# A last scan behind the products with its gates, and a load behind a score: one reordering in an mLSTM and mixture-of-experts kernel

## The chip, the cores and the metric

The kernel runs on one core of one Trainium2 chip. The metric is device time in microseconds (us) of one execution. TensorE (PE) does the matrix products, VectorE (DVE), ScalarE (ACT) and GpSimd (POOL) the elementwise work, and SyncE (SP) issues the transfers between device memory and the core.

## The reference

The inputs are those of an mLSTM layer (2 batches, 8 heads, 768 steps, head size 40) and of a mixture of 4 experts that runs on its output (1536 tokens of 320 values, hidden size 1024).

```python
for t in range(S):
    m_new = np.maximum(f_gate[:, :, t] + m, i_gate[:, :, t])
    f_stab = np.exp(f_gate[:, :, t] + m - m_new)
    i_stab = np.exp(i_gate[:, :, t] - m_new)
    C = f_stab * C + i_stab * outer(v[t], k[t])
    n = f_stab * n + i_stab * k[t]
    y[t] = sigmoid(o_gate[t]) * (C @ q[t]) / np.maximum(np.abs(n @ q[t]), 1.0)
x = y as (tokens, heads * head size)
p = domain_probs / domain_probs.sum(-1)
for e in range(4):
    out += p[:, e] * (np.maximum(x @ w1[e], 0) @ w2[e])
```

## The kernel before, in words

The recurrence is worked in chunks of 128 steps. A chunk of one batch has a number n (n = 0 and 1 are the two batches' first chunk, 2 and 3 their second, and so on), and the chunks 2j and 2j+1 are pair j; there are six pairs. Inside a chunk the work is split into two halves of 64 steps. For pair j the steps are, by the names in the code:

- `load_f` brings the forget factors of a pair from device memory into the tile `fb`, four transfers a pair; `decay(n)` is a scan of VectorE that makes of `fb` the running products `dd` of chunk n. The scan reads `fb` and a constant, `id8`, both in SBUF.
- `values(n)` and `keys(n)` are GpSimd products of the loaded tile `vk` (scaled values `vp`, scaled keys `kp`); `keys(n)` needs the scan of chunk n.
- `scores` are products on TensorE; `weigh(j)` multiplies them on VectorE by `dd` into `pm`, in two halves.
- `carry`, `state` and `keep` pass the state `cs` on: GpSimd, TensorE and VectorE in turn.
- `inter(j)` forms on TensorE the part of the output that comes from the state (`y1`, line 556) and scales it by the decay into `yb`. For j = 1 alone the scaling is split: one VectorE instruction (line 562) for half 0, and eight ScalarE instructions (line 571) for half 1. `intra(j)` forms the part inside the chunk (`y0`, line 596).
- `norms(j)` adds `yb` to `y0` (line 603), makes the denominator (line 604), multiplies by the output gates in `acc` (line 607, tile `xm`), and its second part, `norm(...)`, divides (lines 611 to 654) into `xr`. `gate_o(j)` is the sigmoid on ScalarE that makes those gates, line 390.
- `turn(j)` transposes `xr` on TensorE (tile `px`, line 662) and stores it as `xst`, the input of the experts (ScalarE lines 665 and 666, VectorE lines 669 and 670).

`steps(n)` puts n steps of the first expert between these: a hidden block (TensorE line 157, ScalarE line 166, VectorE line 170) or an output block (TensorE line 204). From about 100 us on only the experts are left.

Nothing reorders this: each engine runs its instructions in the order in which the code emits them, and waits, in order, for what they need. SyncE too issues its transfers in the order of the code. `behind(ap)` is a tiny transfer (line 710, to `mark`) that reads `ap`; SyncE waits until `ap` is written, and so all later transfers stand behind it.

The change touches `inter` and the first round, j = 1, of the loop over pairs. In it `decay(b + 2)` is the scan of chunk 5 (that of chunk 4 stands ahead of the loop), `keys(b + 2)` the keys of chunk 5, and `load_f(3)` the factors of chunks 6 and 7, whose scans run in the round after.

Of the kernel before, what the change touches and what calls it, by code (L numbers as in the profile page):

```python
# [15 lines left out]
B, H, S, D = 2, 8, 768, 40  # L16
NE, DM, FF = 4, 320, 1024
NT = B * S
L = 128
# [4 lines left out]
NP = H // 2  # L24
# [20 lines left out]
def tile_mlstm_moe(ctx, tc, g0, g1, qk, vk, ot, dp, w1, w2, out):  # L45
    ctx.enter_context(tc.manual_schedule())
    nc = tc.nc
# [175 lines left out]
    with ExitStack() as actx:  # L223
# [50 lines left out]
        bT = const.tile([L, 2, NC, B * NP], F32, name="bT")  # L274
# [119 lines left out]
        fbs, dds, vvs, pms, ss, sts = {}, {}, {}, {}, {}, {}  # L394
# [26 lines left out]
        def load_f(j):  # L421
            for n in (2 * j, 2 * j + 1):
                b, c = n % B, n // B
                fbs[n] = fb = a0.tile([L, H, C], F32, tag="fb", name="fb")
                for u in range(2):
                    nc.sync.dma_start(
                        fb[hs[u]].rearrange("p h t -> p (h t)"),
                        f_d[2 * c - 4 + u:2 * c - 3 + u, b * H * C:(b + 1) * H * C].to_broadcast(
                            [C, H * C]
                        ),  # L430
                    )
# [7 lines left out]
        def decay(n):  # L439
            b, c = n % B, n // B  # L440
            if c:
                if not b:
                    d = a1.tile([L, B, H, C], F32, tag=f"dd{c % 2}", name="dd")
                    dds[n], dds[n + 1] = d[:, 0], d[:, 1]
                    dds[c, "pair"] = d
                scan(dds[n], fbs.pop(n), id8)
                return
            dds[n] = a1.tile([L, H, L], F32, tag=f"dd{n}", name="dd")
            for i, f in enumerate(fbs.pop(n)):
                scan(dds[n][:, 4 * i:4 * i + 4], f, id4)  # L450
# [8 lines left out]
        def keys(n):  # L459
            nc.gpsimd.tensor_mul(  # L460
                kp[n % 2][:, :, 0:D], vks[n // 2][:, n % 2, 1],
                dds[n][:, :, (C if n // B else L) - 1:].to_broadcast([L, H, D]),
            )
# [49 lines left out]
        def cst(j, u):  # L513
            return cs[(2 * j + u) % 3]
# [32 lines left out]
        def inter(j, eng=nc.scalar):  # L547

            y1 = ps_a.tile([L, 2, B, NP, C], F32, tag="a", name="y1")
            for n in (2 * j, 2 * j + 1):  # L550
                b = n % B
                for p in range(NP):
                    for r in range(2):
                        q = slice(64 * r, 64 + D * r)
                        for u in (r, 1 - r):
                            nc.tensor.matmul(  # L556
                                y1[hs[u ^ r], r, b, p, 0:D + 1], qT(n)[q, p, hs[u]],
                                cst(j, u)[q, b * NP + p], start=True, stop=True,
                            )
            yb = ybs[j] = a1.tile([L, 2, B, NP, D + 1], F32, tag="yb", name="yb")  # L560
            if eng is nc.vector:
                eng.tensor_mul(  # L562
                    yb[:, 0].rearrange("t b p d -> t (b p) d"),
                    y1[:, 0].rearrange("t b p d -> t (b p) d")[..., 0:D + 1],
                    bT[:, 0, j].unsqueeze(2).to_broadcast([L, B * NP, D + 1]),
                )
            for b in range(B):
                for p in range(NP):
                    for r in range(eng is nc.vector, 2):
                        i = b * NP + p  # L570
                        nc.scalar.activation(  # L571
                            yb[:, r, b, p], y1[:, r, b, p, 0:D + 1], AF.Copy,
                            scale=bT[:, r, j, i:i + 1],
                        )

        def intra0(b):
            pool, tag = (ps_a, "a") if b else (ps_h, "ph")
# [36 lines left out]
        xms, nqs = {}, {}  # L614
# [87 lines left out]
        def steps(n):  # L702
            for _ in range(n):
                if not work[0].step():
                    work.pop(0)

        def behind(ap):

            i = next(marks)
            nc.sync.dma_start(mark[i:i + 1, 0:ap.shape[-1]], ap)  # L710
# [34 lines left out]
        for r in range(2):  # L745
            for u in range(2):
                t = tri[hs[u], r, hs[u ^ r]]
# [113 lines left out]
        for j in range(1, NG):  # L861
            a, b = 2 * j, 2 * j + 1
            nxt, far = j + 1 < NG, j + 2 < NG
            k = SLOTS[j - 1]
            if j == NG - 2:
                raw1 = raws.tile([L, 3, FF], F32, tag="raw", name="raw1")

            def load(i, ap):
                if far or j == NG - 2:
                    behind(ap)  # L870
                if far:
                    (load_vk, None, lambda j: (load_qk(j), load_o(j)))[i](j + 2)
                elif j == NG - 2:
                    nc.sync.dma_start(raw1[:, i], w1[1, :, i])

            if nxt:
                values(a + 2)
                values(b + 2)
                if j > 1:
                    decays(j + 1)  # L880
                else:
                    decay(b + 2)
                keys(a + 2)
                keys(b + 2)
                steps(1)
            if j == 2:
                gate_o(2)
            norm = norms(j)
            if j == 1:
                behind(xms.pop(j)[0:1, 1, 0, 0:32])  # L890
                load_f(3)
            else:
                load(0, xms.pop(j)[0:1, 1, 0, 0:32])
                steps(1)
            norm(nc.vector if j == 1 else nc.gpsimd)
            if j == 1:
                steps(1)
            if nxt:
                carry(j + 1, 0)
            if j == 1:  # L900
                scores(a + 2)
                scores(b + 2)
                weigh(j + 1)
            steps(k[0] - 1 - nxt)
            if j > 1:
                turn(j)()
            if nxt:
                if j > 1:
                    gate_o(j + 1)
                if j > 1:  # L910
                    scores(a + 2)
                    scores(b + 2)
                hidden = work[0].todo[0][0] == work[0].hidden
                state(j + 1, *((ps_o, "po") if hidden else (ps_h, "ph")))
                if j == 1:
                    low = turn(j)
                keep(j + 1, 0)
                if j == 1:
                    load(0, cst(j + 1, 1)[0:1, 0, 0:32])
                    load_o(2)  # L920
                if not far:
                    load(1, cst(j + 1, 1)[0:1, 0, 0:32])
                low() if j == 1 else weigh(j + 1)
                if far:
                    carry(j + 1, 1)
                    keep(j + 1, 1)
                steps(k[1])
                inter(j + 1)
                load(2, ybs[j + 1][0:1, 0, 0, 0, 0:32])
                intra(j + 1)  # L930
# [113 lines left out]
```

## Time and profile before

| What | Value |
|---|---|
| median of 3 runs | 393.89 us (393.89 to 394.18) |
| the profiled execution | 393.9 us, its span 392.2 us |
| TensorE busy | 385.0 us, 98% of the span |
| VectorE, ScalarE, GpSimd busy | 158.8, 123.7, 94.0 us |
| granted TensorE clock, mean | 0.998 |

The span runs from the first to the last instruction of the profiled execution. Its own time is 1.7 us more. The profile has a timeline of each engine (start, duration, operation and, in brackets, the idle time ahead of it and what ended it), the windows (busy time and transfer rate of a stretch) and a view of one line's instructions. A timeline row that merges several instructions gives their number as x8.

### The profile page before, as it was taken

How to read it: one execution, taken by the hardware profiler on the slowest of the kernel's cores; microseconds unless marked ns; L12 is line 12 of the kernel's file. 1: busy time of each engine (PE TensorE's matmuls, PEld its weight loads, DVE VectorE, ACT ScalarE, POOL GpSimd, SP SyncE). 2: the span in 40 equal slices, each digit the busy share in tenths (PEclk: the TensorE clock that was granted, in tenths of full speed). 3: DMA queues.
4: the chain of work that ended last, by engine and by line, in shares of the span. 5: the costliest groups of instructions: out<-in, count | busy, mean ns of one | idle time of the engine just before them, and what ended most of it. 6: DMA issues, size and time to landing. Idle time of an engine off the chain costs nothing.

```text
span 392.2 us, 8247 instructions
## 1 busy us (share of the span) xinstructions
PE 385.0 (98%) x3584; PEld 350.5 (89%) x3584; DVE 158.8 (41%) x270; ACT 123.7 (32%) x296; POOL 94.0 (24%) x114
## 2 busy tenths in 40 slices
PE   9999899999999999999999999999999999999996
PEld 6899799999989989989889889889889899899896
DVE  7788976665433132142141351241231431321421
ACT  3784644446263231061130240160220420310310
POOL 8988344370463100044100010071000100000000
PEclk9999999999999999999999999999999999999999
DMA  7894574353003220003000040003000001001001
GB/s 224 287 289 163 191 228 160 106 198 104 9 1 134 73 89 2 0 2 134 0 2 0 2 160 2 1 0 135 0 2 0 2 8 43 17 17 52 0 18 50
DMA packets 8717, 28.46 MB, mean 73 GB/s; under 512 B 1354, under 2 KB 2906, under 8 KB 7530
## 3 DMA queue, kind: packets, MB, share of 16 engines
q1 hardware_dynamic: 8682, 27.95, 21.2%
q8 instruction: 28, 0.46, 0.5%
q14 instruction: 7, 0.06, 0.0%
HBM read 25.94 MB, written 2.00 MB: 71 GB/s over the span
## 4 chain that ended last, share of the span: by engine, by line
PE 89%; DVE 5%; POOL 3%; issue 2%; ACT 0%; POOLq 0%; DVEq 0%
PE po L204 41%; PE ph L157 38%; PE ph L187 3%; PE pwm L71 1%; PE y L596 1%; PE s L481 1%; POOL w2s L92 1%; PE px L662 1%; PE y L556 1%; PE fb L416 1%; DVE dd L434 1%; DVE xm L607 1%; POOL vp L456 0%; PE st L529 0%; POOL xr L650 0%
## 5 line engine op out<-in xcount | busy, mean ns | idle before, releaser
L204 PE MATMUL po<-w2s,h 128*128 128x320 f32 x1152 | 172.4, 309 | 0.0
L204 PEld LDWEIGHTS po<-w2s,h 128*128 128x128 f32 x1152 | 169.8, 188 | 1.0
L157 PE MATMUL ph<-xst,w1s 128*128 128x512 f32 (+1 forms) x816 | 163.1, 358 | 0.0
L157 PEld LDWEIGHTS ph<-xst,w1s 128*128 128x128 f32 x816 | 135.8, 189 | 24.3 <-issue 2.4
L166 ACT ACTIVATE h<-ph 128x512 fp32r<-128x512 f32 x96 | 57.4, 598 | 191.0 <-PE ph L157 187.5
L170 DVE SCALAR_TENSOR_TENSOR h<-ph,h 128x512 fp32r<-128x512 f32 x96 | 66.3, 691 | 105.8 <-ACT h L166 105.3
L215 DVE SCALAR_TENSOR_TENSOR acc<-po,pw,acc 128x320 f32<-128x320 f32 x36 | 19.8, 550 | 99.9 <-PE po L204 99.9
L92 POOL TENSOR_TENSOR w1s<-raw,w1s 128x512 fp32r<-128x512 f32 (+1 forms) x24 | 23.5, 1029 | 76.1 <-ACT w1s L89 70.9
L92 POOL TENSOR_TENSOR w2s<-raw,w2s 128x640 fp32r<-128x640 f32 x6 | 9.5, 1576 | 96.2 <-ACT w2s L89 96.2
L434 DVE TENSOR_TENSOR_SCAN dd<-fb,id 128x512 f32<-128x512 f32 x14 | 18.9, 1378 | 1.3 <-POOL kp L460 1.0
L571 ACT ACTIVATE yb<-y,bT 128x41 f32<-128x41 f32 x72 | 14.0, 340 | 4.9 <-DVE yb L562 2.6
L89 ACT ACTIVATE w2s<-raw 128x640 fp32r<-128x640 f32 x12 | 8.8, 733 | 19.3 <-DMA raw<-in_w 19.3
L213 ACT ACTIVATE acc<-po,pw 128x320 f32<-128x320 f32 x12 | 6.3, 527 | 22.2 <-PE po L204 22.2
L456 POOL TENSOR_TENSOR vp<-vk,iT 128x320 f32<-128x320 f32 x12 | 11.1, 944 | 8.8 <-PE y L596 4.2
L650 POOL TENSOR_TENSOR xr<-xm,ni 64x320 f32<-64x320 f32 x9 | 7.6, 848 | 21.5 <-DVE ni L612 21.2
L187 PE MATMUL ph<-xd,w1s 64*128 64x512 f32 x40 | 12.0, 419 | 0.0
L187 PE MATMUL ph<-xst,w1s 64*128 64x512 f32 x40 | 12.0, 418 | 0.0
L89 ACT ACTIVATE w1s<-raw 128x512 fp32r<-128x512 f32 (+1 forms) x24 | 11.2, 517 | 0.0
L460 POOL TENSOR_TENSOR kp<-vk,dd 128x320 f32<-128x320 f32 x12 | 9.8, 827 | 1.3 <-DVE dd L434 1.2
L545 DVE TENSOR_TENSOR cs<-cd,st 40x328 f32<-40x328 f32 x18 | 8.9, 492 | 1.1 <-POOL cd L536 0.7
L187 PEld LDWEIGHTS ph<-xst,w1s 64*128 64x128 f32 x40 | 6.6, 185 | 2.9 <-issue 1.9
L92 DVE TENSOR_TENSOR w2s<-raw,w2s 128x640 fp32r<-128x640 f32 x6 | 5.3, 889 | 9.2 <-ACT w2s L89 9.2
(105 smaller groups left out, 200.7 us busy)
## 6 DMA issues: line engine op xcount, KB each, us to landing
qk<-in_qk SPq DMA_DIRECT2D x4, 1024.0 KB, 4.8
raw<-in_w SPq DMA_DIRECT2D x3, 1280.0 KB, 5.4
vk<-in_vk SPq DMA_DIRECT2D x5, 640.0 KB
raw<-in_w SPq DMA_DIRECT2D x2, 1536.0 KB
qk<-in_qk SPq DMA_DIRECT2D x4, 512.0 KB
fb<-f_d SPq DMA_DIRECT2D x16, 128.0 KB, 6.5
acc<-in_ot SPq DMA_DIRECT2D x6, 320.0 KB, 6.8
out<-acc SPq DMA_DIRECT2D x12, 160.0 KB, 1.8
```

Of the source, the lines that this page charges most:

```text
L89: nc.scalar.activation(hi, raw, AF.Copy)
L92: eng.tensor_sub(lo, raw, hi.bitcast(F32))
L157: nc.tensor.matmul(ph[:, i, :], self.w1s[:, wi, f * L:(f + 1) * L], xst[:, xi, self.t0:self.t0 + n], start=(k == 0 and not self.wide), sto ...
L166: nc.scalar.activation(hh, ph, AF.Relu)
L170: nc.vector.scalar_tensor_tensor(out=hl, in0=ph, scalar=0.0, in1=hh.bitcast(F32), op0=ALU.max, op1=ALU.subtract)
L187: nc.tensor.matmul(self.banks[f][:, 0, :], self.w1s[r, 5, f * L:(f + 1) * L], x, start=True, stop=False,)
L204: nc.tensor.matmul(po, self.hs[f][a][:, sl], ws[:, b, f, :], start=(first and i == 0), stop=(last and i == len(ks) - 1),)
L215: nc.vector.scalar_tensor_tensor(out=acc[:, i, :], in0=po, scalar=pw[:, i, e:e + 1], in1=acc[:, i, :], op0=ALU.mult, op1=ALU.add,)
L434: nc.vector.tensor_tensor_scan(out=out.rearrange("p h t -> p (h t)"), data0=f.rearrange("p h t -> p (h t)"), data1=i.rearrange("p h t -> p ...
L456: nc.gpsimd.tensor_mul(vv[:, :, 0:D], vks[n // 2][:, n % 2, 0], iec.to_broadcast([L, H, D]))
L460: nc.gpsimd.tensor_mul(kp[n % 2][:, :, 0:D], vks[n // 2][:, n % 2, 1], dds[n][:, :, (C if n // B else L) - 1:].to_broadcast([L, H, D]),)
L571: nc.scalar.activation(yb[:, r, b, p], y1[:, r, b, p, 0:D + 1], AF.Copy, scale=bT[:, r, j, i:i + 1],)
```

## The change

It does three things. In `inter`, where the scaling is split, the eight ScalarE instructions are emitted ahead of the VectorE instruction. In round j = 1, `decay(5)` and `keys(5)` move from ahead of `norms(1)` to behind its first part. And `load_f(3)` moves from behind `xm` of pair 1 to behind `pm` of pair 2.

```diff
@@ inter(j, eng)
             yb = ybs[j] = a1.tile([L, 2, B, NP, D + 1], F32, tag="yb", name="yb")
-            if eng is nc.vector:
-                eng.tensor_mul(yb[:, 0] ..., y1[:, 0] ..., bT[:, 0, j] ...)
             for b in range(B):
...
                             yb[:, r, b, p], y1[:, r, b, p, 0:D + 1], AF.Copy,
                             scale=bT[:, r, j, i:i + 1],
                         )
+            if eng is nc.vector:
+                eng.tensor_mul(yb[:, 0] ..., y1[:, 0] ..., bT[:, 0, j] ...)
@@ loop over pairs
                 if j > 1:
                     decays(j + 1)
-                else:
-                    decay(b + 2)
                 keys(a + 2)
-                keys(b + 2)
+                if j > 1:
+                    keys(b + 2)
                 steps(1)
...
             norm = norms(j)
             if j == 1:
-                behind(xms.pop(j)[0:1, 1, 0, 0:32])
-                load_f(3)
+                decay(5)
+                keys(5)
             else:
...
             if j == 1:
                 scores(a + 2)
                 scores(b + 2)
                 weigh(j + 1)
+                behind(pms[a + 2][0:1, 0, 0:32])
+                load_f(3)
```

On VectorE, from the scan of chunk 4 to the division of pair 1, the rows stand as follows before and after. The scan is named SCALAR_TENSOR_TENSOR on line 434 here and TENSOR_TENSOR_SCAN in the trace; `y_633` is `y1`, `y_676` is `y0`.

```order
 L434 SCALAR_TENSOR_TENSOR dd<-fb,id_120 128x512 [waits DMAHW4_49,DMAHW3_49]
-L562 TENSOR_TENSOR yb<-y_633,bT 128x328 [waits PE_49]
-L434 SCALAR_TENSOR_TENSOR dd<-fb,id_120 128x512 [waits DMAHW6_49,DMAHW5_49]
-L603 TENSOR_TENSOR y_676<-y_676,yb 128x16x41 [waits DVE_49,PE_49,Activation_49]
+L570 TENSOR_TENSOR yb<-y_633,bT 128x328 [waits PE_49,Activation_49]
+L603 TENSOR_TENSOR y_676<-y_676,yb 128x16x41 [waits DVE_49,PE_49]
 L604 TENSOR_SCALAR nq<-y_676 128x16 [waits DVE_49]
 L607 TENSOR_TENSOR xm<-y_676,acc 128x640
+L434 SCALAR_TENSOR_TENSOR dd<-fb,id_120 128x512 [waits DMAHW6_49,DMAHW5_49]
 L611 TENSOR_TENSOR y_676<-y_676,nq 128x16 [waits DVE_49]
 L612 RECIPROCAL ni<-y_676 128x16 [waits DVE_49]
```

The second scan moved down past three rows, and the scaling on VectorE now waits for ScalarE's eight, where those waited for it before.

On SyncE, at the end of round j = 1's first half, this is the difference; the four `fb` transfers are those of `load_f(3)`.

```order
 L710 DMA mark<-h 1x32
 L377 DMA qk_132<-in_qk 128x2048
-L710 DMA mark<-xm 1x32
+L710 DMA mark<-pm 1x32
 L426 DMA fb<-f_d 64x512 x4
 L710 DMA mark<-cs_131 1x32
```

The order of SyncE's transfers is the same; what the four loads, and all behind them, wait for has moved from `xm` to the first half of `pm`. The orders of TensorE, ScalarE and GpSimd don't move; on ScalarE the first of the eight waits for TensorE instead of VectorE.

## Rows read from the trace of the kernel before

**Rows 1.** Timeline of TensorE: start, duration, operation, idle time ahead.

```profile
32.45 1.14 PE L556 MATMUL y<-cs,qk 64*64 64x41 f32 x64
...
40.66 0.36 PE L529 MATMUL st<-vp,kp 64*40 64x41 f32 x16 [0.43 <-issue]
41.92 0.85 PE L662 MATMUL px<-ident,xr 128*128 128x128 f32 x6 [0.90 <-DVE xr L650]
...
45.65 1.14 PE L596 MATMUL y<-vp,pm 64*64 64x41 f32 x64 [0.35 <-DVE xst L670]
46.73 8.06 PE L157 MATMUL ph<-xst,w1s 128*128 128x256 f32 x64
54.87 0.87 PE L662 MATMUL px<-ident,xr 128*128 128x128 f32 x6
```

**Rows 2.** Timeline of VectorE, the pair's products and the next pair's xm.

```profile
33.65 1.52 DVE L434 TENSOR_TENSOR_SCAN dd<-fb,id 128x512 f32<-128x512 f32 x1
35.21 0.50 DVE L562 TENSOR_TENSOR yb<-y,bT 128x328 f32<-128x328 f32 x1
35.63 2.75 DVE L434 TENSOR_TENSOR_SCAN dd<-fb,id 128x512 f32<-128x512 f32 x1
38.30 0.82 DVE L603 TENSOR_TENSOR y<-y,yb 128x656 f32<-128x656 f32 x1
...
39.25 0.81 DVE L607 TENSOR_TENSOR xm<-y,acc 128x640 f32<-128x640 f32 x1
...
40.60 0.49 DVE L647 TENSOR_TENSOR xr<-xm,ni 128x320 f32<-128x320 f32 x1
41.10 0.67 DVE L650 TENSOR_TENSOR xr<-xm,ni 64x80 f32<-64x80 f32 x1
41.80 0.69 DVE L499 TENSOR_TENSOR pm<-s,dd 128x512 f32<-128x512 f32 x1
...
51.14 0.81 DVE L607 TENSOR_TENSOR xm<-y,acc 128x640 f32<-128x640 f32 x1
```

**Rows 3.** Timeline of GpSimd beside it.

```profile
35.20 1.40 POOL L456 TENSOR_TENSOR vp<-vk,iT 128x320 f32<-128x320 f32 x2
36.57 0.74 POOL L460 TENSOR_TENSOR kp<-vk,dd 128x320 f32<-128x320 f32 x1
38.52 0.74 POOL L460 TENSOR_TENSOR kp<-vk,dd 128x320 f32<-128x320 f32 x1 [1.22 <-DVE dd L434]
40.71 0.96 POOL L650 TENSOR_TENSOR xr<-xm,ni 64x320 f32<-64x320 f32 x1 [1.45 <-DVE ni L612]
...
48.34 1.09 POOL L456 TENSOR_TENSOR vp<-vk,iT 128x320 f32<-128x320 f32 x1 [3.50 <-DMA vk<-in_vk]
```

**Rows 4.** Source view of line 434: duration in ns, least, median and most.

```profile
L434 DVE TENSOR_TENSOR_SCAN dd<-fb,id x14: 1198/1224/2753, 6.1 to 81.0; 128x512 f32<-128x512 f32 x14
```

**Rows 5.** Timeline of ScalarE: the split scaling, a hidden block, pair 2's sigmoid.

```profile
35.80 1.60 ACT L571 ACTIVATE yb<-y,bT 128x41 f32<-128x41 f32 x8 [2.60 <-DVE yb L562]
...
48.94 0.60 ACT L166 ACTIVATE h<-ph 128x512 fp32r<-128x512 f32 x1 [0.22 <-PE ph L157]
49.44 0.73 ACT L390 ACTIVATE acc<-acc 128x640 f32<-128x640 f32 x1
```

**Rows 6.** Timeline of SyncE's queue: when each transfer was issued.

```profile
40.09 0.24 SPq L710 DMA_DIRECT2D mark<-xm  x1
40.38 2.37 SPq L426 DMA_DIRECT2D fb<-f_d  x4
...
43.86 0.36 SPq L383 DMA_DIRECT2D vk<-in_vk  x1
44.27 0.85 SPq L386 DMA_DIRECT2D acc<-in_ot  x1
```

**Rows 7.** Windows: length; PE, PEld, DVE, ACT, POOL; clock, DMA share, GB/s.

```profile
41.00:48.00 7.00, 5.75 (x157) 5.44 (x155) 6.78 (x14) 5.59 (x26) 2.15 (x3) 1.00 0.69 215
46.00:56.00 10.00, 9.92 (x145) 9.40 (x141) 7.84 (x14) 5.96 (x22) 5.56 (x7) 1.00 0.99 319
```

More of the change, by code (lines that the diff above doesn't have):

```diff
@@ L560, in inter @@
             yb = ybs[j] = a1.tile([L, 2, B, NP, D + 1], F32, tag="yb", name="yb")
-            if eng is nc.vector:
[L562 to L566, printed above, removed]
             for b in range(B):
@@ L574, in inter @@
                         )
+            if eng is nc.vector:
+                eng.tensor_mul(
+                    yb[:, 0].rearrange("t b p d -> t (b p) d"),
+                    y1[:, 0].rearrange("t b p d -> t (b p) d")[..., 0:D + 1],
+                    bT[:, 0, j].unsqueeze(2).to_broadcast([L, B * NP, D + 1]),
+                )
         def intra0(b):
```

## The prediction

> **What bounds the kernel now.** I read the page first: TensorE is busy for 98% of the span, so an edit pays only where TensorE stands idle. Then its timeline around the edit [rows 1]. It waits 0.43 us inside the state products (put down to issue, not to another engine), 0.90 us ahead of the transposes of pair 1 at 41.92 (for VectorE's line 650), and 0.35 us ahead of the next `y0` at 45.65 (VectorE's line 670). From there it is all but full: 9.92 of 10 us in the window from 46 to 56 [rows 7]. So what matters is when VectorE gets through its products between 35 and 45 us, and whether TensorE can then use the time.
>
> VectorE's timeline [rows 2] shows the cause: the scan of chunk 5 takes 2.75 us, from 35.63 to 38.38, where the median of 14 scans is 1.22 us [rows 4]. Beside it GpSimd runs three products without a gap, from 35.20 to 37.31 [rows 3], and the scan ends 1.07 us behind the last of them. So the scan hardly ran until GpSimd stopped; 1.5 us of it is waiting, and the addition of line 603, queued behind it, starts only at 38.30. The Trainium skill states this as a rule ("SBUF — State Buffer", section "Who interferes with whom"): a VectorE instruction with two SBUF inputs and a GpSimd instruction that reads SBUF share an interface, and the later one blocks for the whole of the other. By it the scan would end near 37.31 + 1.22 = 38.53; the trace has 38.38 and agrees.
>
> **The change part by part.** No operation is added or removed; three move.
>
> The eight ScalarE instructions first. Before, ScalarE stood idle for 2.60 us until VectorE's half was written, and began 0.09 us behind its end (35.71 to 35.80) [rows 2, 5]. Now it needs only `y1`, whose products end at 32.45 + 1.14 = 33.59 [rows 1]; with the same 0.09 it begins at 33.68 and ends 1.60 us later, at 35.28. VectorE's half, in turn, now waits for all eight: 35.28 + 0.09 = 35.37, against 35.21 before. This costs 0.16 us on VectorE, with nothing to hide it, since the scan of chunk 4 ends at 35.17. Behind the waiting instruction stands all of VectorE's chain.
>
> The scan behind the products. The half scaling takes 0.50 us, to 35.87. The addition follows at about 35.90 instead of 38.30, and from its start to the end of `xm` it is 40.06 - 38.30 = 1.76 us [rows 2]: 37.66. This stretch overlaps GpSimd's three products, and I cost that at nothing: VectorE's half scaling, which like these instructions takes one operand from PSUM, kept to 0.50 us right beside GpSimd. The upper bound is 1.5 us, what the scan lost. Then the scan, at 37.66, when GpSimd is through at 37.31 and waits for this very scan: 1.22 us, to 38.88. The division's line 647 came 40.60 - 40.06 = 0.54 us behind `xm`; now it is ready 0.54 us behind the scan, at 39.42, 1.18 us earlier.
>
> A part of this goes back at once. The keys of chunk 5 start 0.14 us behind the scan (38.38 to 38.52) and take 0.74 [rows 3]: 39.02 to 39.76, later than before by 0.50. Line 647 reads two SBUF tiles as the scan does, so it may wait for them, till about 39.65 (the scan, too, went on a little ahead of GpSimd's recorded end). From line 647's start to line 650's end it was 1.17 us: 40.82 instead of 41.77. If line 647 isn't held, it is 40.59. I take 40.82, the value by the scan's row: **0.95 us** earlier. The rule of the skill named above speaks against the change here: by it the keys, which start first, hold line 647 to their end; without it the gain would be 1.18 us. GpSimd's part of the division (0.96 us from 39.85) ends by 40.82 as well. The state products, which need these keys, end at 41.02 as before [rows 1]; the transposes can start then, 0.90 us earlier, and the rest of VectorE's row follows without a gap, so the `y0` products come at about 44.7 instead of 45.65.
>
> The load. SyncE's mark waited for `xm`, and issued at 40.09 [rows 6]. Now it waits for the first half of `pm`, which starts with the chain at 41.80 - 0.95 = 40.85 and takes 0.69: 41.54. The mark and four loads then need 42.75 - 40.09 = 2.66 us: to 44.23 instead of 42.75. Behind them in SyncE's queue stand the mark on `cs`, `vk` of pair 3 and the gates `acc` of pair 2. They waited for `cs` until 43.5; now they wait for the loads. With 0.24 us for a mark and some gaps, `vk` is issued near 44.6 instead of 43.86 and `acc` near 45.0 instead of 44.27: **0.75 us** later each. The transfers are themselves short of room: their share is 0.99 from 46 to 56 us, after 0.69 from 41 to 48 [rows 7], so what starts later lands later. I take 0.75 us for the landings; the bounds are 0.3 (what straggles now may then run freely) and 1.45 (the loads' own shift).
>
> Who waits for that? The sigmoid of pair 2, ahead of `xm` at 51.14. `vk` had landed by 48.34, where it ended GpSimd's wait [rows 3]. `acc`, 128 x 640 values of 4 bytes or 328 KB, issued right behind it, needs 1.03 us at the 319 GB/s of the window; from about 48.2 this gives 49.2, between 48.3 and the sigmoid's start at 49.44 [rows 5, 7]. Later by 0.75 this is 49.95; the sigmoid, 0.09 behind it and 0.73 long, ends at 50.77. Without the loads `xm` of pair 2 would start at 51.14 - 0.95 = 50.19. So it starts near 50.80, and the gain there is 0.34 us. The transposes of pair 2 at 54.87 follow from it, TensorE's 8.06 us of hidden blocks having ended earlier: more than half of what TensorE saved it then waits there. GpSimd's four products with `vk` (about 2.9 us from 49.0 on) end at 52.0, just ahead of the division, and cost nothing; without that cover they would cost what they overrun. The factors themselves land by 47.7 now, since their scan of chunk 7 ran at 47.7 without a wait; 1.45 later the scan still ends near 49, when the first hidden block's VectorE part is ready.
>
> **Sum.** 0.95 us less at `y0` of pair 2, 0.6 given back at `xm` of pair 2, 0.35 left. Behind 55 us TensorE is full, so what is left stays to the end: 393.9 - 0.35 = 393.55 for the profiled execution, whose 393.9 is also the median. Something over 0.2% of this, 0.8 us, is about what a measurement can tell from no change; this is less.
>
> **Rivals.** (a) All of it is kept: `acc` lands by 50.19 - 0.73 - 0.09 = 49.37, less than 0.2 us later than now. For it speaks that its landing is read here from bounds a whole us apart; against it, the full transfer engines and the later issue. 393.9 - 0.95 = 392.95. (b) The scan is slow by itself or for another neighbour, such as ScalarE's eight, and takes its 2.75 us wherever it stands: then it ends at 40.41, the keys at 41.29, line 650 at 42.4, 0.6 later than before, and with the loads behind it (`acc` 2.3 later, 51.4, sigmoid to 52.2) `xm` of pair 2 comes 1.1 us late: 395.0. The 13 other scans, of which the median is 1.22, speak against it. (c) Slower by the same block in the next pair: if the factors of chunk 7 land behind `vk` of pair 3, GpSimd's first three products (2.1 us) run ahead of that scan and hold it to 51.2, end 52.4 instead of 48.9; the hidden block's VectorE part and `xm` wait behind it, some 2.8 us: 396.7. It decides when the factors land later than about 49.0; they are issued ahead of `vk`, which speaks against it. (d) The change doesn't do what it says, and the addition still comes late, because ScalarE's eight begin late: 393.9.
>
> **How the numbers follow.** Forecast, with the larger part given back: 0.59, and 393.1 to 394.3 as its own range (landings 0.3 to 1.45 later give a gain of 0.8 to a loss of 0.35, with a little more for the products that TensorE reads next, whose transfer stands in the same queue). (a) 0.23, faster by over 0.2%. (b) 0.07 and (c) 0.06, slower. (d) 0.05, the same. So faster 0.23, same 0.64, slower 0.13. The range takes in (a), the forecast's own range and a little of what lies between it and (b): 392.8 to 394.6.
>
> **What would show it.** Right: the scan of chunk 5 at about 1.2 us, starting near 37.7; the addition near 35.9; ScalarE's eight from 33.7; transposes of pair 1 near 41.0; `fb` loads from 41.8; TensorE idle for some 0.6 us ahead of the transposes of pair 2, put down to the division there, and ScalarE's sigmoid waiting for `acc`. Wrong: a scan over 2 us, line 647 late by a whole chain of GpSimd's, no wait at the sigmoid (then a), or scan 7 stretched beside GpSimd (then c).

## The result, and the profile after

The changed kernel takes 396.85 us, the median of 6 runs (395.35 to 397.44); the kernel before, beside it, 394.16 (6 runs, 393.89 to 394.78). The ratio is 1.0062, with a 95% interval of 1.0043 to 1.0081: slower by 0.6%, where 393.55 was forecast and 394.6 was the upper end of the range. A ratio is estimated over all executions but those more than 1.5% above the fastest of the same kernel (four of twelve in one kernel, with everything early), so it need not be the quotient of the two medians. The profiled execution took 396.73 us, 2.8 more than that of before.

The first half of the forecast came about nearly to the hundredth. VectorE's timeline of the changed kernel (start, duration, operation, idle time ahead and its releaser), which answers to [rows 2]:

```profile
35.33 0.50 DVE L570 TENSOR_TENSOR yb<-y,bT 128x328 f32<-128x328 f32 x1 [0.16 <-ACT yb L565]
35.93 0.85 DVE L603 TENSOR_TENSOR y<-y,yb 128x656 f32<-128x656 f32 x1
...
37.64 1.21 DVE L434 TENSOR_TENSOR_SCAN dd<-fb,id 128x512 f32<-128x512 f32 x1
...
39.26 0.82 DVE L647 TENSOR_TENSOR xr<-xm,ni 128x320 f32<-128x320 f32 x1
40.09 0.67 DVE L650 TENSOR_TENSOR xr<-xm,ni 64x80 f32<-64x80 f32 x1
...
52.73 0.82 DVE L607 TENSOR_TENSOR xm<-y,acc 128x640 f32<-128x640 f32 x1 [2.53 <-ACT acc L390]
53.47 0.68 DVE L170 SCALAR_TENSOR_TENSOR h<-ph,h 128x512 fp32r<-128x512 f32 x1
```

The scan takes 1.21 us instead of 2.75, and line 650 ends at 40.76 (forecast 40.82). The last two rows are the trouble: `xm` of pair 2 comes at 52.73 instead of 51.14 [rows 2], behind an idle stretch of 2.53 us. TensorE's timeline of the same kernel, against [rows 1]:

```profile
40.90 0.85 PE L662 MATMUL px<-ident,xr 128*128 128x128 f32 x6 [0.54 <-DVE xr L650]
...
44.63 1.14 PE L596 MATMUL y<-vp,pm 64*64 64x41 f32 x64 [0.35 <-DVE xst L670]
45.70 6.01 PE L157 MATMUL ph<-xst,w1s 128*128 128x256 f32 x48
54.21 3.11 PE L157 MATMUL ph<-xst,w1s 128*128 128x256 f32 x16 [2.49 <-DVE h L170]
57.12 1.48 PE L662 MATMUL px<-ident,xr 128*128 128x128 f32 x6
```

At the `y0` products TensorE is 1.02 us ahead of before (44.63 against 45.65). Then the 64 products of the four hidden blocks, which ran as one row of 8.06 us, break after the third block for 2.49 us, and what follows is slow: 3.11 us for the fourth block, 1.48 for transposes that took 0.87. These start 2.25 us later than before (57.12 against 54.87) and last 0.61 longer, together 2.86 us: all of the loss. What the break waits for is told by the chain of waits (start, length, what) in that stretch:

```profile
45.19 6.75 DMA acc<-in_ot
...
51.96 0.74 ACT acc L390
...
52.73 0.82 DVE xm L607
53.55 0.61 DVE h L170
...
54.21 3.11 PE ph L157 x16
```

The gates of pair 2 are issued at 45.19 and land 6.75 us later. ScalarE's sigmoid waits for them, VectorE's `xm` for the sigmoid, the second hidden block's VectorE part stands behind `xm` in VectorE's row, and TensorE's fourth block needs that. ScalarE's timeline shows the same, against [rows 5]:

```profile
33.70 1.60 ACT L565 ACTIVATE yb<-y,bT 128x41 f32<-128x41 f32 x8 [0.52 <-PE y L556]
...
47.92 0.60 ACT L166 ACTIVATE h<-ph 128x512 fp32r<-128x512 f32 x1 [0.22 <-PE ph L157]
51.96 0.74 ACT L390 ACTIVATE acc<-acc 128x640 f32<-128x640 f32 x1 [3.45 <-DMA acc<-in_ot]
52.60 1.07 ACT L166 ACTIVATE h<-ph 128x512 fp32r<-128x512 f32 x2
```

And SyncE's queue, against [rows 6], shows the gates issued 0.92 us later (45.19 against 44.27):

```profile
41.51 0.24 SPq L710 DMA_DIRECT2D mark<-pm  x1
41.80 2.38 SPq L426 DMA_DIRECT2D fb<-f_d  x4
44.28 0.40 SPq L710 DMA_DIRECT2D mark<-cs  x1
44.77 0.36 SPq L383 DMA_DIRECT2D vk<-in_vk  x1
45.19 0.42 SPq L386 DMA_DIRECT2D acc<-in_ot  x1
```

The slow products are told by the windows (length; PE, PEld, DVE, ACT, POOL busy; granted clock, DMA share, GB/s):

```profile
51.70:54.20 2.50, 0.02 (x1) 0.00 (x0) 1.47 (x3) 1.71 (x3) 2.39 (x4) 1.00 0.99 333
54.00:55.00 1.00, 0.79 (x6) 0.80 (x7) 0.93 (x5) 0.00 (x0) 0.39 (x2) 1.00 0.92 196
55.00:56.00 1.00, 1.00 (x7) 1.00 (x6) 0.66 (x2) 0.00 (x0) 0.94 (x2) 0.53 0.91 244
56.00:57.00 1.00, 1.00 (x7) 1.00 (x6) 0.00 (x0) 0.00 (x0) 0.92 (x2) 0.50 1.10 256
57.00:58.00 1.00, 1.00 (x7) 0.96 (x7) 0.01 (x1) 0.60 (x1) 0.23 (x1) 0.50 0.69 219
58.00:59.00 1.00, 1.00 (x33) 0.62 (x35) 0.68 (x1) 0.36 (x2) 0.00 (x0) 0.76 0.15 61
```

TensorE stood idle from 51.70 to 54.20, and from 55 to past 58 us its granted clock was half (1.2 GHz instead of 2.4).

### The profile page after: what moved, and what is told of

Its sections match the earlier page's. It is cut to its first block, busy times and chain, and to the rows that moved or that the text cites. A ratio compares the mean times of both kernels' runs of the same rounds, so it can differ in the third digit from the quotient of the medians.

```text
span 395.0 us, 8247 instructions
## 1 busy us (share of the span) xinstructions
PE 385.9 (98%) x3584; PEld 351.5 (89%) x3584; DVE 157.7 (40%) x270; ACT 123.6 (31%) x296; POOL 93.5 (24%) x114
## 4 chain that ended last, share of the span: by engine, by line
PE 91%; DVE 5%; DMA 2%; issue 1%; ACT 1%; SPq 0%; POOL 0%; DVEq 0%; POOLq 0%; ACTq 0%
PE po L204 42%; PE ph L157 40%; PE ph L187 3%; DMA acc<-in_ot 2%; PE s L481 1%; PE y L556 1%; PE px L662 1%; DVE dd L434 1%; PE y L596 1%; PE fb L416 1%; PE st L529 1%; DVE xm L607 1%; ACT yb L565 0%; DVE pm L489 0%; PE s L476 0%
## 5 line engine op out<-in xcount | busy, mean ns | idle before, releaser
L434 DVE TENSOR_TENSOR_SCAN dd<-fb,id 128x512 f32<-128x512 f32 x14 | 17.3, 1264 | 1.4 <-POOL kp L460 1.0
L536 POOL TENSOR_TENSOR cd<-cs,bl 104x328 f32<-104x328 f32 x9 | 6.6, 736 | 10.7 <-DVE cs L545 10.3
```

Source lines behind the costliest of these rows:

```text
L434: nc.vector.tensor_tensor_scan(out=out.rearrange("p h t -> p (h t)"), data0=f.rearrange("p h t -> p (h t)"), data1=i.rearrange("p h t -> p ...
```

## The experiments

In the first runs theory A says that the loss comes from the moved load, by the gates. Its rivals are named with the runs. All times in a heading are medians; the ratio is to the kernel before beside it. The label of each stands in brackets.

**The load put back** (e1_load_back, and once more as e9_load_back_again), in the changed kernel:

```diff
                 decay(5)
                 keys(5)
+                behind(xms.pop(j)[0:1, 1, 0, 0:32])
+                load_f(3)
...
-                behind(pms[a + 2][0:1, 0, 0:32])
-                load_f(3)
```

> The changed kernel with one of its three parts undone: the load of the fourth pair's factors stands behind xm of pair 1 again; the scan and the keys stay behind the products, ScalarE's eight stay first. Theory A (the moved load is the whole loss, the moved scan is a gain): xm of pair 1 is ready near 37.7, so the loads are issued near 37.8 instead of 40.4, the gates of pair 2 land no later than in the kernel before, TensorE keeps the 0.95 us at the next y0 (44.7) and has no idle time of over 0.3 us ahead of the transposes of pair 2: 392.8 to 393.3. Rival B (the moved scan and the earlier TensorE are themselves what costs, by meeting the transfers at another time): still slower than before, 395 or more.

393.83 us, ratio 1.0011 (0.9994 to 1.0028). The sigmoid ran at 49.44 without a wait, so the loss is gone with the load. But the gain did not come either; theory A had expected it. TensorE's timeline of this kernel shows where it went:

```profile
44.94 0.67 PE L596 MATMUL y<-vp,pm 64*64 64x41 f32 x30 [0.36 <-DVE xst L670]
46.08 0.72 PE L596 MATMUL y<-vp,pm 64*64 64x41 f32 x34 [0.47 <-issue]
```

The `y0` products start 0.7 us earlier than before and stop after 30 of 64, for nothing that another engine does ("issue"). The trace's transfer records have a packet of TensorE's instructions (16 KB, one packet of the queue named instruction) from 43.46 to 44.78; TensorE goes on 1.30 us behind its end. That they are TensorE's is read from the counts: the 28 such packets of a run are 64 bytes for each of TensorE's 3,584 products and 3,584 weight loads, and the page counts under 300 instructions on any other engine. So the next limit stood 0.7 us behind the one that was removed: TensorE's own instructions.

> The changed kernel with the factors' load put back, a second time, for a second profile. Theory P (the gain at the output products is lost or kept by when TensorE's own instruction packets come): if the packet falls near 41 and 46 us, the products inside pair 2 run without a gap and the second transposes start near 54.2 instead of 54.88; if it falls near 44 us, there is again a gap of 0.5 to 1.3 us inside those products and they start at 54.9 or later. Theory Q (the gain is always lost): 54.9 in any case. Both: no wait of the sigmoid for the gates (start 49.5 or earlier), and a median of 393.2 to 394.2 us.

393.84 us, ratio 0.9997 (0.998 to 1.0013). The packet fell at 43.18 again, with the same gap of 0.47 us, and the second transposes started at 54.59, 0.28 us earlier than in the first profile of before and 0.06 later than in its second (54.53, below). The early kind of packet that the expectation wanted to see did not occur. Nothing can be told between the two theories from this alone, but no gain can be measured.

**The load alone** (e2_load_only), in the kernel before:

```diff
-                behind(xms.pop(j)[0:1, 1, 0, 0:32])
-                load_f(3)
+                pass
...
                 weigh(j + 1)
+                behind(pms[a + 2][0:1, 0, 0:32])
+                load_f(3)
```

> The kernel before with only the load moved: behind pm of pair 2 (42.5 in that kernel) instead of xm of pair 1 (40.1). Theory A: the gates of pair 2 are issued near 46.2 instead of 44.3 and land at 51 to 53 instead of about 49; the sigmoid, xm of pair 2 and TensorE's fourth hidden block wait for them: 395 to 397.5. Rival B: the load by itself costs nothing: 393.7 to 394.3.

395.05 us, ratio 1.0038 (1.0020 to 1.0056). In the profiled execution (396.79) the sigmoid waited 2.87 us for the gates, to 52.38, and TensorE stood for 1.91 us ahead of the fourth hidden block. The load alone makes a loss: 1.2 us between the medians, against 2.7 for the changed kernel and 1.5 for it in a second batch, and not in every execution (393.94 to 397.18).

**ScalarE's half first, alone** (e5_act_first): the change in `inter` on the kernel before. Theory G says that GpSimd holds the scan of chunk 5; the rival is ScalarE's eight instructions beside it.

> The kernel before with one part alone: ScalarE's eight instructions ahead of VectorE's half of the scaling. ScalarE is then through near 35.3, ahead of the scan of chunk 5 at about 35.9, while GpSimd's three products run beside the scan as before. Theory G (GpSimd's products hold the scan): the scan still ends near 38.4, 1.0 to 1.1 us behind GpSimd's third product, and the time stays within 0.2%: 393.5 to 394.3. Rival S (ScalarE's eight beside it stretch the scan): the scan takes about 1.2 us, VectorE's chain is 1.3 us earlier, 392.7 to 393.2.

393.86 us, ratio 0.9993 (0.9973 to 1.0012). ScalarE's eight were through by 35.38, and yet, on VectorE and on GpSimd:

```profile
35.83 2.54 DVE L434 TENSOR_TENSOR_SCAN dd<-fb,id 128x512 f32<-128x512 f32 x1
...
36.56 0.73 POOL L460 TENSOR_TENSOR kp<-vk,dd 128x320 f32<-128x320 f32 x1
```

The scan ends at 38.37, 1.08 us behind GpSimd's last product (36.56 + 0.73 = 37.29); before it was 1.07. Theory G stands. It is the rule on the shared interface of VectorE and GpSimd in the Trainium skill ("SBUF — State Buffer", section "Who interferes with whom"), and the two runs agree with it. A run further down (e14_qk_first), which keeps the order of before on VectorE and GpSimd, has the reverse: its scan of chunk 5 took 1.45 us, from 35.10, and GpSimd's two products with line 456, begun at 34.75, took 2.32 us instead of 1.40.

**The gates issued first** (e3_gates_early): in the changed kernel `load_o(2)` goes ahead of the factors.

```diff
                 weigh(j + 1)
                 behind(pms[a + 2][0:1, 0, 0:32])
+                load_o(2)
                 load_f(3)
...
-                    load_o(2)
```

> The changed kernel with one transfer moved: the gates of pair 2 are issued ahead of the fourth pair's factors, right behind the third pair's queries and keys (near 32) instead of behind vk of pair 3. Theory A1 (the wait is for the gates): the sigmoid of pair 2 runs at 48.5, TensorE's fourth hidden block doesn't wait, and what is late next is GpSimd with vk of pair 3, which still lands 1 to 3 us later than in the kernel before, so the transposes of pair 2 come between 54 and 55.7: 393.3 to 395. Theory A2 (the whole queue of transfers is late, and vk alone costs as much as the gates did): 396 or more.

395.23 us, ratio 1.0043 (1.0021 to 1.0066); the profiled execution took 394.13. The sigmoid did not wait (49.47). But `vk` came late (GpSimd's products at 50.61 instead of 48.34), the `y0` products broke for 0.67 us, and the second transposes came at 55.17. Theory A1 was right on the wait and on the transposes; the median lies above its range and below that of A2.

**`vk` and the gates first: both behind `xm` of pair 1, the factors behind `pm`** (e6_vk_gates_first), in the changed kernel:

```diff
                 keys(5)
+                load(0, xms.pop(j)[0:1, 1, 0, 0:32])
+                load_o(2)
...
-                if j == 1:
-                    load(0, cst(j + 1, 1)[0:1, 0, 0:32])
-                    load_o(2)
```

> The changed kernel with two transfers moved: vk of pair 3 and the gates of pair 2 are issued behind xm of pair 1 (37.8), ahead of the fourth pair's factors, which stay behind pm of pair 2. Theory A (the loss is the late landing of these two): both land by 43, nobody waits for them, and TensorE has no idle stretch between the hidden blocks; with the moved scan's 0.95 us kept 392.8 to 393.3. Theory A with a second limit, which the kernel with the load put back showed (TensorE 0.7 us early at the y0 products, then 0.47 us idle inside them, put down to issue, some 1.3 us behind the end of a 16 KB instruction packet): the same without the 0.95 us, 393.5 to 394.2. Rival (the moved factors alone are late enough to cost, by the scans of chunks 6 and 7): 395 or more.

396.77 us, ratio 1.0058 (1.0037 to 1.0079). No engine waits for `vk` or the gates any more, and the kernel is as slow as the changed one. VectorE's scans waited 1.13 us for the factors, to 46.73; TensorE waited for none of this:

```profile
44.72 0.67 PE L596 MATMUL y<-vp,pm 64*64 64x41 f32 x30 [0.35 <-DVE xst L670]
46.68 1.19 PE L596 MATMUL y<-vp,pm 64*64 64x41 f32 x34 [1.29 <-issue]
47.79 10.24 PE L157 MATMUL ph<-xst,w1s 128*128 128x256 f32 x64
```

An instruction packet from 44.35 to 45.38, a gap of 1.29 us up to 1.30 us behind it, and half clock from then to about 53 us (10.24 us for what took 8.06).

**Everything early** (e7_all_early, and e10_all_early_again): factors, `vk` and the gates all behind `xm` of pair 1, in the changed kernel.

```diff
                 keys(5)
+                behind(xms.pop(j)[0:1, 1, 0, 0:32])
+                load_f(3)
+                load_vk(3)
+                load_o(2)
```

> The changed kernel with the factors of the fourth pair, vk of pair 3 and the gates of pair 2 all issued behind xm of pair 1 (37.8 to 41.5), in this order. Theory A: no wait for any of them; what TensorE then keeps depends on whether its instruction packets come in time: 392.8 to 393.3 if they do, 393.5 to 394.2 if they wait behind this denser traffic. Rival (transfers in one dense stretch land later than spread out and somebody waits): 394.5 or more.

397.4 us (12 executions, 392.71 to 402.24), ratio 1.0036 (1.0001 to 1.0070). The profiled execution, 393.34, is what the change was meant to give:

```profile
44.62 1.14 PE L596 MATMUL y<-vp,pm 64*64 64x41 f32 x64 [0.34 <-DVE xst L670]
45.69 8.36 PE L157 MATMUL ph<-xst,w1s 128*128 128x256 f32 x64
54.13 0.88 PE L662 MATMUL px<-ident,xr 128*128 128x128 f32 x6
```

No gap, no wait, the second transposes 0.74 us earlier than before. Of the 1.03 us at `y0`, 0.3 went in the hidden blocks, which took 8.36 us instead of 8.06; VectorE's scans of chunks 6 and 7, now beside GpSimd's products, took 3.26 us instead of 2.34. Its instruction packets came at 40.89 and 46.29, not near 44.

> All of pair 3's loads and the gates ahead of the second score, a second time, since its executions lay from 392.7 to 402 us and only one of 393.3 was profiled. Theory P: with the packet near 41 and 46 us again 54.1 at the second transposes and an execution of 393.3; with it near 44 us a gap inside the output products, half clock behind it as with the gates alone, and 396 to 398. Rival: the spread comes from another place, then transposes at 54.1 and an execution over 395.

398.16 us (393.27 to 398.63), ratio 1.0108 (1.0091 to 1.0125). The profiled execution was again a short one (393.27, transposes at 54.24, packets at 41.24 and 45.79). What the others lose their 4 to 5 us to is not in any profile. A part can be read from the granted clock that is on record for each execution as a mean: 0.990 or 0.991 in the four long ones, 0.999 in the short one. The difference, some 0.008 of 397 us, is about 3 us of work at full clock (an estimate, if TensorE was busy then). In the first batch the eight executions over 397 us have 0.989 to 0.996, the four others 0.998 or more. What lowered the clock stays open.

**Warming products** (e4_dummies, and e11_dummies_again): in round 2 of the changed kernel three extra products of 512, 512 and 128 columns stand ahead of the fourth hidden block, so that TensorE is busy there. Theory C says that the idle stretch makes the half clock.

> The changed kernel with three products of zeros (512, 512 and 128 columns, into a PSUM tile that nobody reads) on TensorE between the third and the fourth hidden block of round 2, where the changed kernel's TensorE stands idle for 2.49 us and its granted clock falls to half from 55.1 to 58.5. Theory C (about 1.4 us of the loss is the half clock, not the wait): the dummies run inside the wait, the clock stays at full speed, 395.0 to 395.6. Rival D (the clock falls for another reason than the idle stretch, or the dummies don't fit into the wait): 396.5 or more.

397.07 us, ratio 1.0086 (1.0058 to 1.0113).

> The changed kernel with three warming products in TensorE's queue ahead of the last hidden block of round 2, a second time, since the first execution had no wait for the gates. If this one has it (sigmoid near 51 to 52): theory C (clock price follows from the idle stretch) expects clock 1.0 from 54 to 58 us, the hidden block's 16 products in 2.1 to 2.3 us and an end 0.5 to 1.5 us ahead of the first changed run's 396.7; rival: half clock all the same, 3.1 us. If it has no such wait, nothing follows.

One execution, 397.09. Both are inconclusive for theory C: neither had the wait for the gates. Both had a packet near 44.5 and a gap in the `y0` products (1.29 and 1.02 us) with half clock behind it, ahead of the place that was to be tried. The products themselves lengthen TensorE's row by some 1.9 us (55.27 to 57.13 in the first), so the times say nothing on it either. The runs served for something else: in both the gates, issued at 46.34 and 45.55, landed by 51.02 and 50.05, only 4.68 and 4.50 us later.

**The same two kernels again** (e8_changed_again, e12_before_again).

> The changed kernel once more, for a second profiled execution and more times. Theory A (the late gates are what this order of transfers does): the sigmoid of pair 2 waits for its transfer again, TensorE stands idle for 1 us or more ahead of the fourth hidden block, 395.5 to 397.5. Rival H (the landing at 51.9 was one execution's, made by one instruction packet of 1.8 us at 46.9 among the transfers): the sigmoid runs by 50.9 with no such idle stretch, and the times spread down to 394.

395.58 us, ratio 1.0035 (1.0016 to 1.0055). The wait recurs, but shorter; ScalarE and TensorE in an execution of 394.48:

```profile
51.02 0.74 ACT L390 ACTIVATE acc<-acc 128x640 f32<-128x640 f32 x1 [2.35 <-DMA acc<-in_ot]
...
53.27 2.17 PE L157 MATMUL ph<-xst,w1s 128*128 128x256 f32 x16 [1.40 <-DVE h L170]
```

> The kernel before, a second time. Theory P: if its packet falls near 41 and 46 us, the state products run without the issue idle of 0.43 us, and the second transposes still start at 54.8 to 54.9, since the output products wait for the division of pair 1 there; an execution of 393.5 to 394. Rival: it gains 0.5 us or more by the earlier packet, and then the timing of the packet, not the change, makes part of the differences.

393.53 us, packet at 43.48 again, second transposes at 54.53.

**What makes the gates late?** Theory S: the 1 MB of `qk` of pair 3, which is issued at 46.04 whatever the change does, now follows the gates by 0.85 us instead of 1.82 and shares the engines with them. Theory R: the late issue and the instruction packet alone. Three runs move the `qk`: in the changed kernel behind a hidden block of round 2 (e13_qk_later), in the kernel before to just ahead of `vk` (e14_qk_first), and in the changed kernel behind `xm` of pair 1 (e15_qk_early). The lines shown are those that came in; `load_qk(3)` goes at its old place.

```diff
@@ e13_qk_later, round 2
             if j == 2:
+                behind(work[0].made.bitcast(F32))
+                load_qk(3)
+                load_o(3)
                 gate_o(2)
@@ e14_qk_first, round 1
+                    load_qk(3)
                     load_vk(3)
                     load_o(2)
@@ e15_qk_early, round 1
                 keys(5)
+                behind(xms.pop(j)[0:1, 1, 0, 0:32])
+                load_qk(3)
```

> The changed kernel, but qk and the gates of pair 3 are issued behind the first hidden block of round 2 (about 48.6 us) instead of behind yb (46.04). Theory S (the gates of pair 2 land late because the 1 MB of qk, issued 0.85 us behind them, shares the engines): the gates land by 49, ScalarE's sigmoid runs without a wait, TensorE has no idle stretch ahead of the last hidden block, and the scores start at 55.7 or earlier instead of 58.53 (unless the qk itself now comes late for them, which would show as a wait for it there); median 393.5 to 394.5. Theory R (late issue and instruction packet alone): the sigmoid still waits to 51 or 52, median 395.5 to 397.

396.97 us, ratio 1.0069 (1.0044 to 1.0094). Theory S falls: with no `qk` before 50.81 the gates were later than ever. Chain, ScalarE and TensorE:

```profile
45.18 8.03 DMA acc<-in_ot
...
53.24 0.74 ACT L390 ACTIVATE acc<-acc 128x640 f32<-128x640 f32 x1 [4.70 <-DMA acc<-in_ot]
...
55.48 3.69 PE L157 MATMUL ph<-xst,w1s 128*128 128x256 f32 x16 [3.74 <-DVE h L170]
```

A transfer signals in 16 parts. Of these gates 15 were there by 50.32 and the last came at 53.21; of `vk` 15 by 48.88, the last at 52.43. So one part of each came 2.89 and 3.55 us behind the other fifteen. The time of an instruction packet is read from its row among the DMA queues (packets, MB, share of 16 engines). In the window from 45.8 to 48.7 us, first this kernel, then the changed one, then the one before:

```profile
q8 instruction: 1, 0.02, 5.8%
```

```profile
q8 instruction: 1, 0.02, 3.9%
```

```profile
q8 instruction: 1, 0.02, 2.1%
```

5.8% of 16 engines over 2.9 us is 2.69 us for one packet of 16 KB, 3.9% is 1.81 us, 2.1% is 0.97 us, near what most packets of a run take (0.88 to 1.5).

> The kernel before, with qk of pair 3 issued right ahead of vk and the gates (about 43.9) instead of behind yb (46.09); the factors stay where they were. Theory S: the gates, now behind 1 MB more, land 2 to 3 us later than the 49.1 of before, the sigmoid waits to 51 or 52, and the time is 395 to 397. Theory R: the issue of the gates moves by only 0.4 us, so no wait over 0.5 us, and the time is 393.7 to 394.3.

397.46 us, ratio 1.0102 (1.0036 to 1.0167). The sigmoid waited to 52.94, as S said: 1 MB ahead of the gates makes them late. That is a price of that order, not the cause in the changed kernel. Here, too, the last part of the gates came late, at 52.92, 1.13 us behind the 15th, although the packet among these transfers (from 49.62) took only 0.93 us. In TensorE's row:

```profile
55.19 2.17 PE L157 MATMUL ph<-xst,w1s 128*128 128x256 f32 x16 [2.62 <-DVE h L170]
```

> The changed kernel with qk of pair 3 issued behind xm of pair 1 (about 38.0), into engines that stood nearly empty from 38 to 42 us; the factors stay behind pm. Theory S: no wait for the gates, second scores at 55.0 to 55.7, 393.2 to 394.0, unless the instruction packet falls late, then a gap in the output products and up to 396. Theory R: the sigmoid waits as in the changed kernel (to 51 or 52), 395.5 to 397.

395.4 us, ratio 1.0045 (1.0024 to 1.0066). No wait for the gates, which landed 4.52 us behind their issue; but that was so in the warming runs too, where `qk` stood where it was, and in all three the packet fell near 44.4 instead of 46. So it doesn't speak for S. TensorE:

```profile
44.90 0.67 PE L596 MATMUL y<-vp,pm 64*64 64x41 f32 x30 [0.35 <-DVE xst L670]
46.86 0.72 PE L596 MATMUL y<-vp,pm 64*64 64x41 f32 x34 [1.29 <-issue]
47.51 8.07 PE L157 MATMUL ph<-xst,w1s 128*128 128x256 f32 x64
```

Put together, from the landing records of the profiled executions that have the factors behind `pm` and the gates behind `vk`:

| Kernel | packet near 46 (us long) | gates issued | 15 parts by | last part | end of the wait or of the gap | second transposes |
|---|---|---|---|---|---|---|
| changed | 46.87 (1.80) | 45.19 | 50.65 | 51.94 | wait, TensorE 2.49 idle | 57.12 |
| changed, again | 46.14 (2.16) | 45.32 | 50.45 | 51.00 | wait, 1.40 idle | 55.53 |
| load alone | 46.91 (2.16) | 46.15 | 51.33 | 52.35 | wait, 1.91 idle | 57.17 |
| qk later | 45.89 (2.69) | 45.18 | 50.32 | 53.21 | wait, 3.74 idle | 59.01 |
| warming | none (44.86) | 46.34 | 50.72 | 51.02 | gap in `y0`, 1.29 | 59.13 |
| warming, again | none (44.17) | 45.55 | 49.79 | 50.05 | gap in `y0`, 1.02 | 58.13 |
| qk early | none (44.39) | 45.80 | 50.16 | 50.32 | gap in `y0`, 1.29 | 55.66 |

(The warming runs' 59.13 and 58.13 have the extra products in them.) In these seven a packet comes either near 46, and then takes 1.80 to 2.69 us and one sixteenth of the gates comes late; or between 44.2 and 44.9, and then TensorE runs out of instructions in the `y0` products. The five kernels that were profiled twice showed the same kind both times. In the kernel before a packet of usual length (0.97 us, from 47.73) lay among these transfers, and the last part of the gates came only 0.10 us behind the 15th. No run has the gates issued as early as before and a long packet among them, so how much of the late landing is the moved load's and how much the packet's is not separated. That the load belongs to the cause is shown by the medians, with it put back and with it alone.

## Why the prediction was wrong

**Right: the scan.** That GpSimd holds the scan of chunk 5, that behind the products it takes 1.2 us, what it costs at line 647 (which took 0.82 instead of 0.49, to 40.08, behind keys that run from 38.99 to 39.73), and the 0.95 us at `y0` (measured 1.02): each at the row and by the step that the prediction named; that GpSimd holds the scan is confirmed by the run with ScalarE's half alone. One step was wrong without harm: the state products, put at "41.02 as before", ended at 40.36, since the `issue` stretch of [rows 1] did not occur, and the transposes waited for line 650.

**Wrong, and the step that failed: "I take 0.75 us for the landings".** The gates landed 2.86 us later than before (51.94 against 49.08; that the loss at the transposes is 2.86 too is chance) and 1.92 us later in the second profile; the bounds, 0.3 to 1.45, were too narrow as well. The issue itself came 0.92 us later, about as forecast, and with no packet in the way the landing follows the issue by 4.50 to 4.68 us, as in the two warming runs and the run with `qk` early: 45.19 + 4.5 to 4.7 = 49.7 to 49.9, the 49.95 of the forecast. What came on top has two parts. The first fifteen parts of the gates took 5.13 to 5.46 us from the issue in the four profiles with a packet near 46, against 4.24 to 4.38 in the three without; and the 16th part came 0.55 to 2.89 us behind the 15th, against 0.16 to 0.30 in those three and 0.10 in the first profile of before. That this packet is the cause is argued from these seven profiles and not shown: no run moved the packet alone, the delay does not grow with the packet (0.55 us with one of 2.16, 1.29 with one of 1.80), and a last part came 1.1 to 1.4 us late beside a packet of usual length as well (the gates of `qk` first; a transfer of the factors in the first profile of before, 45.88 behind 44.44). The Trainium skill ("DMA: Bandwidth & Descriptors", section "Why a DMA increments its semaphore by 16 and not by 1") says that the data of a transfer are there only when the last of its engines has signalled. The waits agree: the sigmoid starts 0.02 or 0.03 us behind the last part (51.96 and 51.94, 53.24 and 53.21), not behind the 15th. On which engine a packet lay, no record here shows.

**The price of the wait was right, its place was not.** I let the wait hold only `xm` and the second transposes, "TensorE's 8.06 us of hidden blocks having ended earlier". They had not ended: the second block's ScalarE and VectorE parts stand behind the sigmoid and `xm` in their engines' rows (52.60 and 53.47), and TensorE's fourth block, which needs them, starts 2.25 us behind the sigmoid (54.21 behind 51.96, 53.27 behind 51.02; 2.24 or 2.25 in the three other runs with this wait). TensorE's third block ends at 51.71, so every sigmoid later than 51.71 - 2.25 = 49.46 costs TensorE its delay beyond that. With the forecast's landing the sigmoid starts at 49.95 + 0.09 = 50.04, and TensorE would have stood 0.58 us ahead of the fourth block instead of some 0.6 ahead of the transposes: the same sum at another place. Measured, `xm` came 1.59 us late, and at full clock the transposes would have come 1.60 late (54.21 + 2.26 = 56.47, where 2.26 is the way from 53.27 to 55.53 in the second execution).

**Not foreseen: the clock.** Half clock after the idle stretch took 0.65 us up to the transposes (57.12 instead of 56.47) and 0.61 in them. With these 1.26 us the account closes: the profiled execution is 3.18 us over the forecast (396.73 against 393.55), 1.92 by the sigmoid (51.96 instead of 50.04) and 1.26 by the clock. The two profiled executions of the changed kernel, 396.73 and 394.48, differ by the idle stretch (2.49 and 1.40) and by this. The 16 executions of the changed kernel on record agree: the seven with a mean granted clock of 0.999 or more took 394.31 to 396.45 us (median 395.35), the nine with 0.990 to 0.996 took 395.71 to 397.44 (median 396.73). No experiment isolated it: theory C stays untried.

**Not foreseen: the gain isn't safe either.** I had costed TensorE's own row at nothing once VectorE was early. The `issue` stretch of 0.43 us in [rows 1] was the sign. With the load put back, or with `vk` or the gates issued earlier, TensorE came 0.7 to 1.0 us earlier to the `y0` products and ran out of instructions inside them for 0.47 to 1.29 us. Only the kernel with everything early kept a gain, about 0.6 us in its two profiled executions (393.34 and 393.27 against 393.9); two more of its 17 executions were as short (392.71, 392.83), and the other 13 were slower than the kernel before, by up to 2%. So none of these versions beats the kernel before by a measurable amount.

Of the rivals, (a) failed with the landing. (b) had nearly the right times for the gates and the end (sigmoid to 52.2, 395.0), by luck: its reason, a scan that stays slow, did not occur. (c) did not occur: the scans of chunks 6 and 7 ran in 2.34 us together, from 45.55, without a stretch. (d) did not occur.

**Open:** what decides whether the packet comes near 44 or near 46, how much of the late landing the packet makes, and why the clock is lower in the long executions of the kernel with everything early. The two kinds part ahead of the moved load: where a packet comes near 46, an earlier one came at 35.5 to 36.3 us, in the other kernels at 37.8 to 39.2. With the load alone it came at 36.21, against 38.00 and 37.85 in the kernel before, though the two kernels do the same up to 40 us.

## What to carry to other kernels

A load that is moved to a later place is paid for by what stands behind it in the transfer queue: list those transfers, take the time from issue to landing as it is in the trace with a spread, and ask for each of them what stands behind the instruction that waits for it on its engine, and from which moment the bounding engine stands. Before a stretch ahead of the bounding engine is shortened, look at what else comes to it at that time: an `issue` stretch near the place says that its own instructions are only just in time.

## What the runs showed of the hardware

- The instructions of TensorE come in packets of 16 KB, 28 in a run, which the profile counts to the same 16 engines as the data. Most took 0.88 to 1.5 us, the one near 46 us 1.8 to 2.7 among full transfers of the changed order; where one came late, TensorE's `y0` products went on 1.2 to 1.5 us behind its end (46.34 behind 45.13, 46.08 behind 44.78, 46.86 behind 45.39).
- A single part of a transfer can come 3.55 us behind the other fifteen (`vk` with `qk` later, 52.43 behind 48.88).
- How long TensorE stood idle does not by itself tell whether its clock falls: it was halved after gaps of 1.02 and 1.29 us in the `y0` products (warming runs, `vk` and the gates first) and after 1.91, 2.49 and 3.74 us ahead of the fourth block; it stayed at full speed after 1.29 us in the same products (`qk` early) and after 1.40 and 2.62 us ahead of the fourth block (changed kernel again, `qk` first). Between `vk` and the gates first and `qk` early, both with 1.29 us, the four hidden blocks took 10.24 and 8.07 us: 2.17 us is the price of half clock there.
